# Reordering the second stage of a fused attention and feed-forward kernel: scaling of w_out among block transposes, an earlier load of batch 2's v, and second scores one step later

## The chip, the cores and the metric

The kernel runs on one core of a Trainium2 chip. The metric is the device time of one execution in microseconds (us); the profiled span is about 2 us shorter (287.1 against 288.98 us here). The engines are named as in the profile: PE is the matrix engine (PEld its weight loads), DVE is VectorE, ACT is ScalarE, POOL is GpSimd, SP is SyncE. A "q" after a name means the engine's sequencer, which also issues DMAs.

## The reference, cut to what matters

```python
# attention inside chunks of 64 tokens: 8 batches, 8 heads, 576 tokens, head size 64
scores = scale * np.matmul(q_c, k_c.transpose(0, 1, 2, 4, 3))
attn = softmax(scores)                       # written out in the reference
out = np.matmul(attn, v_c)
x = out.transpose(0, 2, 1, 3).reshape(4608, 512)
# feed-forward: w_in is 512 x 2048, w_out is 2048 x 512
h = x @ w_in
g = h * (1.0 / (1.0 + np.exp(-beta * h)))
return g @ w_out
```

## The kernel before

The tokens go through in nine blocks of 512. For each block PE does a long run of hidden-layer matmuls (`hps`), then the output product. Between them lie the scores (`sc`, 64 tiny matmuls of 32 rows by 64 columns for each group of four chunks) and the attention products (`x`) of the next block. From block 1 on, the output product is a Strassen-like form which needs four precomputed differences of w_out (`tw`); block 0 uses the plain form in 16 units of four wide matmuls: unit number 4g + t uses quarter g of w_out.

Because the activation is written as Silu of beta times h, w_out must be divided by beta first. That is `scale_w_out(g)`, four VectorE instructions for quarter g, called "group g" below. GpSimd issues all loads (they convert float32 to float16 on the way: the page gives 36.71 MB read from HBM and 18.35 MB carried by the loads' queue, q0) and calculates the differences.

```python
def scale_w_out(g):                                    # VectorE, 4 instructions of 128x512 f16
    for kk in range(4 * g, 4 * g + 4):
        nc.vector.tensor_scalar_mul(wo(kk), wo(kk), binv[:, kk % 2, kk // 2:kk // 2 + 1])

def T_items(b):                                        # VectorE: 4 block transposes, q and k of batch b
    return [lambda z=z, w=w: emit_T(b, z, w) for z in range(2) for w in range(2)]

def emit_tw(n):                                        # GpSimd: one weight difference, 128x2048 f16
    # ... tw1 = b12 - b11 (needs groups 0 and 1), tw2 = b22 - tw1 (needs all), tw4 = b21 - tw2, tw3 = b22 - b12
    nc.gpsimd.tensor_tensor(out=o, in0=a_, in1=b_, op=ALU.subtract)
# ...
load_w_out(0); load_w_out(1)                           # one call per line in the kernel
load_qk(1)
load_w_out(2)
load_v(1)
load_w_out(3)
load_qk(2)
# ... attention of block 0, then the hidden layer of block 0:
L1(0, {-2: lambda: emit_xp(2), -3: lambda: emit_xp(3)}, 4)
scale_w_out(0)
scale_w_out(1)
for f in T_items(1):
    f()
scale_w_out(2)
scale_w_out(3)
emit_tw(1)
emit_tw(2)
load_v(2)
load_qk(3)
emit_tw(4)
emit_tw(3)
hooks = {
    9: lambda: emit_sc(2),
    11: lambda: emit_sc(3),
    12: lambda: emit_pv(4, xbar=False),                # attention product, then VectorE normalises it
    13: lambda: [emit_pv(5, xbar=False), emit_xp(4)],
    14: lambda: [emit_pv(6, xbar=False), emit_xp(5)],
    15: lambda: [emit_pv(7, xbar=False), emit_xp(6)],
}
for kk, f in enumerate(L2_plain(0)):                   # the 16 units of block 0's output product
    hooks.get(kk, lambda: None)()
    f()
# ... blocks 1 to 8
```

In the traces of this case each engine runs its instructions in the order in which the program names them (VectorE, for example, starts the four transposes at 33.05, 35.82, 36.92 and 38.00 us and then group 2 of the scaling at 39.08). The order of calls above is therefore the order on each engine.

The softmax here doesn't subtract the row's maximum and nothing guards it: scores larger than these inputs give would overflow.

Of the kernel before, what the change touches and what calls it, by code (L numbers as in the profile page):

```python
# [15 lines left out]
def kernel(  # L16
# [10 lines left out]
    nc = tc.nc  # L27
# [88 lines left out]
    def scale_w_out(g):  # L116
        for kk in range(4 * g, 4 * g + 4):
            nc.vector.tensor_scalar_mul(wo(kk), wo(kk), binv[:, kk % 2, kk // 2:kk // 2 + 1])  # L118
# [15 lines left out]
    def T_items(b):  # L134
        return [lambda z=z, w=w: emit_T(b, z, w) for z in range(2) for w in range(2)]
# [35 lines left out]
    def emit_pv(i, spare=False, xbar=True):  # L171
        g = i // 2
        if spare:
            xs = [ps_p.tile([128, 4, 128], FP32, tag="p", name="xp") for _ in range(2)]
        else:
            x = ps_x.tile([128, 2, 4, 128], FP32, tag="x", name="x")
            xs = [x[:, 0], x[:, 1]]
        for s in range(4):
            z, a2 = s // 2, s % 2
            for hp, cp in ((0, 0), (1, 1), (0, 1), (1, 0)):  # L180
                b, cb = divmod(2 * i + cp, NCB)
                p0, o0 = 64 * hp, 64 * cp
                nc.tensor.matmul(  # L183
                    out=xs[hp][o0:o0 + 64, s, 0:D + 1],
                    lhsT=et_t[g, a2][p0:p0 + 64, z, 2 * (i % 2) + cp, :],
                    rhs=vbuf[b % NV][p0:p0 + 64, s, cb, 0:D + 1],
                )
        rd = rd_p.tile([128, 2, 4, 1], FP32, tag="rd", name="rd")
        x16 = x_p.tile([128, 2, 4, D], FP16, tag="x16", name="x16")
        for xx, rr, yy in (  # L190
            [(xs[h], rd[:, h], x16[:, h]) for h in range(2)] if spare else [(x, rd, x16)]
        ):
            shape = [128] + list(yy.shape[1:])
            if spare:
                nc.vector.reciprocal(out=rr, in_=xx[:, :, D:D + 1])
                src = xx[:, :, 0:D]
            else:
                nc.vector.reciprocal(out=rr, in_=xx[:, :, :, D:D + 1])
                src = xx[:, :, :, 0:D]
            nc.vector.tensor_tensor(  # L200
                out=yy, in0=src, in1=rr.to_broadcast(shape), op=ALU.mult,
            )
        j, t0 = i // 4, (i % 4) * 128
        if j not in xt_t:
            xt_t[j] = xt_p.tile([128, KDM, BLK], FP16, tag="xt", name="xt")
        xf = x16.rearrange("p e s d -> p (e s d)")
        if xbar:
            nc.sync.dma_start_transpose(out=xt_t[j][:, :, t0:t0 + 128], in_=xf)
        else:
            x16_t[i] = xf  # L210

    def emit_xp(i):
        xf = x16_t.pop(i)
        j, t0 = i // 4, (i % 4) * 128
        xps = ps_s.tile([128, KDM, 128], FP16, tag=f"sc{i % 2}", name="xps")
        for kk in range(KDM):
            nc.tensor.transpose(
                out=xps[:, kk, :], in_=xf[:, kk * 128:(kk + 1) * 128], identity=ident
            )
        nc.scalar.copy(out=xt_t[j][:, :, t0:t0 + 128], in_=xps)  # L220

    def emit_idle(n):
        d = ps_p.tile([128, BLK], FP32, tag="p", name="idle")
        for _ in range(n):
            nc.tensor.matmul(out=d, lhsT=zero[:, 0:128], rhs=zero, start=True, stop=True)

    gt_t = {}
    s_t = {}
# [49 lines left out]
    def emit_tw(n):  # L278
        t1, t2, t3, t4 = tw
        w = w_out16.rearrange("p m r d -> p (m r) d")  # L280
        b11, b12 = w[:, 0:NM, 0:HM], w[:, 0:NM, HM:DM]
        b21, b22 = w[:, NM:KFF, 0:HM], w[:, NM:KFF, HM:DM]
        o, a_, b_ = {1: (t1, b12, b11), 2: (t2, b22, t1), 3: (t3, b22, b12), 4: (t4, b21, t2)}[n]
        nc.gpsimd.tensor_tensor(out=o, in0=a_, in1=b_, op=ALU.subtract)
# [172 lines left out]
    with tc.manual_schedule():  # L457
        load_qk(0, split=True)
        nc.vector.memset(zero, 0.0)
        nc.vector.memset(bstage, 0.0)  # L460
        nc.vector.memset(warm, 0.0)
        nc.scalar.activation(out=warm, in_=warm, func=ACTF.Exp, scale=1.0)
        for g4 in range(4):
            nc.sync.dma_start(
                out=bstage[32 * g4:32 * g4 + NM].rearrange("p r i -> p (r i)"),
                in_=moe_beta.rearrange("(m g x) -> g m x", g=4, x=64)[g4],
            )
        for t in vbuf:
            nc.vector.memset(t[:, :, :, D:D + 1], 1.0)
        load_v(0)  # L470
        make_identity(nc, ident)
        for g in range(4):
            load_w_in(g)
        load_w_out(0)
        load_w_out(1)
# [6 lines that stand above are left out]
        emit_idle(4)  # L482
        for f in T_items(0):
            f()
        nc.vector.transpose(
            out=bt, in_=bstage.rearrange("p r i -> p (r i)").rearrange("p (i r) -> p r i", r=2)
        )
        eps = 2.0 ** -10
        nc.vector.tensor_tensor(out=bm, in0=bt, in1=bt, op=ALU.mult)
        nc.vector.tensor_scalar(  # L490
            out=bm, in0=bm, scalar1=eps * eps, scalar2=None, op0=ALU.is_ge)
        nc.vector.scalar_tensor_tensor(
            out=beta2, in0=bt, scalar=eps, in1=bm, op0=ALU.subtract, op1=ALU.mult)
        nc.vector.tensor_scalar_add(beta2, beta2, eps)
        nc.vector.reciprocal(out=binv, in_=beta2)
        emit_sc(0, between=lambda: emit_idle(5))
        emit_sc(1, spare=True)
        emit_idle(3)
        emit_pv(0, xbar=False)
        emit_pv(1, spare=True, xbar=False)  # L500
        emit_xp(0)
        emit_pv(2, xbar=False)
        emit_xp(1)
        emit_pv(3, spare=True, xbar=False)

        L1(0, {-2: lambda: emit_xp(2), -3: lambda: emit_xp(3)}, 4)
        scale_w_out(0)
        scale_w_out(1)
        for f in T_items(1):
            f()  # L510
        scale_w_out(2)
        scale_w_out(3)
        emit_tw(1)
        emit_tw(2)
        load_v(2)
        load_qk(3)
        emit_tw(4)
        emit_tw(3)
        hooks = {
            9: lambda: emit_sc(2),  # L520
            11: lambda: emit_sc(3),
            12: lambda: emit_pv(4, xbar=False),
            13: lambda: [emit_pv(5, xbar=False), emit_xp(4)],
            14: lambda: [emit_pv(6, xbar=False), emit_xp(5)],
            15: lambda: [emit_pv(7, xbar=False), emit_xp(6)],
        }
        for kk, f in enumerate(L2_plain(0)):
            hooks.get(kk, lambda: None)()
            f()

        for j in range(1, NB):
            na = j + 1
            hooks = {}
            if na < NB:
                hooks[KFF] = lambda: emit_sc(2 * na)
            if j == 1:
                T2 = T_items(2)
                hooks.update({-1: lambda: emit_xp(7), 4: T2[0], 7: T2[1], 10: T2[2], 12: T2[3]})
            L1(j, hooks)
            at = []  # L540
            if na < NB:
                at = [
                    lambda: emit_pv(4 * na), lambda: emit_sc(2 * na + 1),
                    lambda: emit_pv(4 * na + 1), lambda: emit_pv(4 * na + 2),
                    lambda: emit_pv(4 * na + 3),
                ]
            tr = T_items(j + 2) if j + 2 < B else []

            def go(lst):
                if lst:  # L550
                    lst.pop(0)()

            mm, cB, cD, cC = steps_L2(j, last=(j == NB - 1))
            mm[0]()
            while fill:
                dve()
            mm[1]()
            cB()
            go(at)
            go(at)  # L560
            emit_sum(j, 4, 0)
            emit_sum(j, 4, 1)
            mm[2]()
            go(tr)
            go(at)
            emit_sum(j, 4, 2)
            emit_sum(j, 4, 3)
            mm[3]()
            go(at)
            go(tr)  # L570
            mm[4]()
            cD()
            go(at)
            go(tr)
            mm[5]()
            if j < NB - 1:
                cC()
            go(tr)
            mm[6]()
            if j + 2 < B:  # L580
                load_v(j + 2)
            if j + 3 < B:
                load_qk(j + 3)
# [30 lines left out]
```

## Time and profile before

| | before |
|---|---|
| median time | 288.98 us (288.88 to 289.02, 4 runs) |
| profiled span | 287.1 us, granted clock 1.00 |
| PE busy | 271.6 us, 95% |
| start of block 0's hidden layer | 17.83 us |
| start of block 1's long hidden-layer run | 55.44 us |
| from there to the end | 231.6 us, PE back to back nearly throughout |

The first lines of the profile's page, and its line for queue 8, which it names instruction:

```profile
span 287.1 us, 7722 instructions
PE 271.6 (95%) x3388; PEld 176.4 (61%) x3388; DVE 140.6 (49%) x261; ACT 161.8 (56%) x240; POOL 117.1 (41%) x114
...
q8 instruction: 26, 0.43, 0.6%
```

The 26 packets of queue 8 carry 0.43 MB, so about 16 KB each.

The waits of PE in the first 100 us. Columns: engine and line that waited, who released it, us in total, times, longest:

```profile
PE sc L155 <- DVE kT L127: 5.4, 1, 5.4
PE ops L405 <- DVE w_out L118: 1.5, 1, 1.5
...
PE x L183 <- issue: 0.6, 1, 0.6
PE sc L155 <- ACT et L164: 0.5, 2, 0.3
```

The change is aimed at the last three. "Issue" means that PE waited for nothing that the profile knows of.

The timeline of the stage. Columns: start, duration, engine, line, operation, count, and in brackets the idle time before it and what ended it. Lines of weight loads (PEld) are left out here and below without a mark; "..." stands for all other lines left out:

```profile
37.04 4.07 POOL L284 TENSOR_TENSOR tw<-w_out 128x2048 f16<-128x2048 f16 x1
...
39.08 2.99 DVE L118 TENSOR_SCALAR w_out<-w_out,binv 128x512 f16<-128x512 f16 x4
41.33 1.16 PE L405 MATMUL ops<-w_out,gt 128*128 128x512 f16 x4 [1.47 <-DVE w_out L118]
...
44.55 1.14 DVE L118 TENSOR_SCALAR w_out<-w_out,binv 128x512 f16<-128x512 f16 x4 [2.49 <-DMA w_out<-in_moe_w_out_dram]
...
47.26 0.22 PE L183 MATMUL x<-vb,et 64*64 64x65 f16 x3
48.05 0.31 PE L183 MATMUL x<-vb,et 64*64 64x65 f16 x13 [0.56 <-issue]
48.29 1.04 PE L405 MATMUL ops<-w_out,gt 128*128 128x512 f16 x4
...
49.46 0.32 PE L183 MATMUL x<-vb,et 64*64 64x65 f16 x16
```

Group 2 of the scaling (39.08) takes 2.99 us for the same four instructions that take 1.14 us as group 3 (44.55). In the trace its first instruction alone lasts 2.20 us and ends at 41.28, which is 0.17 us after GpSimd's difference ends. PE starts unit 8 at 41.33, after 1.47 us of idleness. Unit 12, the first to use the last quarter of w_out, starts at 48.29.

The chain of waits through the same time (start, us, what):

```profile
39.23 2.06 DVE w_out L118
...
41.33 1.16 PE ops L405 x4
...
47.48 0.56 issue
48.05 0.41 PE x L183 x13
...
55.44 13.12 PE hps L240 x64
```

The cut in the middle holds the first scores, a table load of ScalarE (1.28 us from 43.23) and the exps (44.53 to 45.62), for which the second scores waited.

### The profile page before, as it was taken

The page shows a single profiled execution, that of the slowest core. Times are in us where ns is not written, and L with a number is a line of the kernel's source. Part 1 is how long each engine was busy: PE and PEld are TensorE (multiplying, and loading weights), DVE is VectorE, ACT ScalarE, POOL GpSimd, SP SyncE. Part 2 cuts the span into 40 slices and gives each one's busy share as a digit, 9 for nine tenths or more (in the row PEclk, how much of TensorE's full clock was granted, in tenths as well). Part 3 has the DMA queues.
Part 4 walks back from the last instruction along what each step waited for, and adds up shares of the span by engine and source line. Part 5 has one row for each costly group of instructions (what it writes and reads, how often), then busy time and mean ns, then how long its engine had stood idle before and what let it go on. Part 6 is the DMA issues. An engine that isn't in the chain of part 4 may idle for free.

```text
span 287.1 us, 7722 instructions
## 1 busy us (share of the span) xinstructions
PE 271.6 (95%) x3388; PEld 176.4 (61%) x3388; DVE 140.6 (49%) x261; ACT 161.8 (56%) x240; POOL 117.1 (41%) x114
## 2 busy tenths in 40 slices
PE   2779978999999999999999999999999999999995
PEld 0454434546874688468845884588458845885584
DVE  2751483837770677067806680668055404540433
ACT  2249505688348833883388438842884288518710
POOL 8733266994049203920393039302910260016100
PEclk9999999999999999999999999999999999999999
DMA  6999998990239626972597259823902320242013
GB/s 112 177 206 212 211 182 153 184 211 3 75 110 158 130 67 112 159 132 63 105 161 142 59 99 164 154 59 94 154 4 57 94 73 2 57 94 73 2 37 110
DMA packets 69584, 31.95 MB, mean 111 GB/s; under 512 B 53680, under 2 KB 63920, under 8 KB 69552
## 3 DMA queue, kind: packets, MB, share of 16 engines
q0 software_dynamic: 44960, 18.35, 51.9%
q1 hardware_dynamic: 24448, 12.99, 17.4%
q8 instruction: 26, 0.43, 0.6%
q10 hardware_dynamic: 144, 0.13, 0.1%
q14 instruction: 6, 0.05, 0.1%
HBM read 36.71 MB, written 9.44 MB: 161 GB/s over the span
## 4 chain that ended last, share of the span: by engine, by line
PE 82%; DMA 10%; DVE 3%; POOL 2%; issue 1%; ACT 1%; DVEq 0%; POOLq 0%; ACTq 0%
PE hps L240 39%; PE oA L310 20%; DMA ku<-in_k_dram 7%; PE oD L310 5%; PE oB L310 5%; PE oC L310 5%; PE sc L155 4%; PE x L183 3%; DMA vb<-in_v_dram 3%; PE ops L405 1%; DVE kT L127 1%; DVE w_out L118 1%; POOL qu L85 1%; PE oE L310 1%; POOL vb L95 1%
## 5 line engine op out<-in xcount | busy, mean ns | idle before, releaser
L240 PE MATMUL hps<-xt,wi 128*128 128x512 f16 (+1 forms) x656 | 127.8, 353 | 1.2 <-DMA wi<-in_moe_w_in_dram 0.7
L250 ACT ACTIVATE gt<-hps,beta 128x512 f16<-128x512 f32 x144 | 95.8, 688 | 17.8 <-PE hps L240 17.1
L240 PEld LDWEIGHTS <-wi 128*128 128x128 f16 x656 | 63.4, 98 | 61.7 <-DMA xt<-x 1.5
L270 DVE TENSOR_TENSOR s<-gt 128x512 f16<-128x512 f16 x32 | 17.7, 552 | 80.1 <-ACT gt L250 79.9
L355 POOL TENSOR_TENSOR w<-u,u 128x512 f32<-128x512 f32 x7 | 8.9, 1270 | 103.3 <-ACT u L321 103.3
L310 PEld LDWEIGHTS <-s 128*128 128x128 f16 x496 | 46.8, 98 | 6.0
L310 PE MATMUL oA<-tw,s 128*128 128x256 f16 x368 | 44.1, 273 | 0.0
L274 POOL TENSOR_TENSOR s<-gt 128x512 f16<-128x512 f16 x32 | 37.5, 1228 | 4.8 <-ACT gt L250 4.8
L310 PEld LDWEIGHTS <-gt 128*128 128x128 f16 x384 | 36.4, 98 | 4.8
L321 ACT COPY u<-oA 128x512 f32<-128x512 f32 x24 | 14.1, 588 | 37.0 <-PE oA L310 37.0
L164 ACT ACTIVATE et<-sc 128x512 f16<-128x512 f32 x34 | 18.5, 595 | 22.3 <-PE sc L155 22.2
L95 POOL DMA_DIRECT2D vb<-in_v_dram x32 | 27.5, 879 | 6.6 <-DMA wi<-in_moe_w_in_dram 5.0
L200 DVE TENSOR_TENSOR x<-x,rd 128x512 f16<-128x512 f32 x34 | 23.5, 691 | 1.3
L127 DVE STREAM_TRANSPOSE qT<-qu 128x576 f32<-128x576 f32 x16 | 20.0, 1250 | 5.8 <-DMA qu<-in_q_dram 5.8
L127 DVE STREAM_TRANSPOSE kT<-ku 128x576 f32<-128x576 f32 x16 | 19.9, 1241 | 2.1 <-DMA ku<-in_k_dram 2.0
L155 PEld LDWEIGHTS <-kT 32*64 32x64 f16 x1152 | 11.6, 111 | 12.2 <-DVE kT L127 6.3
L155 PE MATMUL sc<-qT,kT 32*64 32x64 f16 x1088 | 12.8, 195 | 6.2 <-DVE kT L127 5.4
L272 DVE TENSOR_TENSOR s<-s,gt 128x512 f16<-128x512 f16 x32 | 17.8, 555 | 1.1
L372 ACT COPY o<-oA 128x512 f32<-128x512 f32 x7 | 4.1, 586 | 23.2 <-PE oA L310 23.2
L405 PE MATMUL ops<-w_out,gt 128*128 128x512 f16 x64 | 15.3, 379 | 1.5 <-DVE w_out L118 1.5
L375 POOL TENSOR_TENSOR o<-t,o 128x512 f32<-128x512 f32 x7 | 8.9, 1270 | 18.0 <-ACT o L372 18.0
L164 ACT ACT_TABLE_LOAD x8 | 10.3, 1283 | 10.0 <-PE sc L155 9.9
(56 smaller groups left out, 208.8 us busy)
## 6 DMA issues: line engine op xcount, KB each, us to landing
out_dram<-osb SPq DMA_DIRECT2D x21, 256.0 KB, 2.2
vb<-in_v_dram POOLq DMA_DIRECT2D x32, 144.0 KB, 4.9
qu<-in_q_dram POOLq DMA_DIRECT2D x7, 576.0 KB, 9.1
ku<-in_k_dram POOLq DMA_DIRECT2D x7, 576.0 KB, 11.1
out_dram<-o SPq DMA_DIRECT2D x14, 256.0 KB, 2.2
wi<-in_moe_w_in_dram POOLq DMA_DIRECT2D x4, 512.0 KB, 12.5
w_out<-in_moe_w_out_dram POOLq DMA_DIRECT2D x4, 512.0 KB, 16.8
qu<-in_q_dram POOLq DMA_DIRECT2D x2, 288.0 KB, 5.3
```

The costliest lines, as they stand in the source:

```text
L95: nc.gpsimd.dma_start(out=t[64 * hp:64 * hp + 64, 2 * z:2 * z + 2, :, 0:D].rearrange("p s c d -> p (s c) d"), in_=v[b, h0:h0 + 2].rearrang ...
L127: nc.vector.transpose(out=dst[b][:, z].rearrange("p t r e -> p (t r e)").bitcast(FP32).rearrange("p (t r) -> p r t", r=RUN), in_=src[b][:, ...
L155: nc.tensor.matmul(out=sc[a % 2][o0:o0 + 64, z, c, :], lhsT=kk[:, cb * CH:(cb + 1) * CH, e], rhs=qq[:, cb * CH:(cb + 1) * CH, e], start=(e ...
L164: nc.scalar.activation(out=et, in_=sc[s], func=ACTF.Exp, scale=scale)
L200: nc.vector.tensor_tensor(out=yy, in0=src, in1=rr.to_broadcast(shape), op=ALU.mult,)
L240: nc.tensor.matmul(out=hps_t[j, m][:, c0:c1], lhsT=w_r[m // 4][:, 2 * z + e, m // 2 % 2, m % 2, :], rhs=xt_t[j][:, n, c0:c1], start=(n == ...
L250: nc.scalar.activation(out=gt_t[j][:, m, :], in_=hps, func=ACTF.Silu, scale=beta2[:, m % 2, m // 2:m // 2 + 1],)
L270: tt(out=s1[:, lo], in0=g[:, lo, dn], in1=g[:, hi, dn], op=ALU.add)
L272: tt(out=s2[:, lo], in0=s1[:, lo], in1=g[:, lo, up], op=ALU.subtract)
L274: tt(out=s3[:, lo], in0=g[:, lo, up], in1=g[:, lo, dn], op=ALU.subtract)
L310: nc.tensor.matmul(out=bank[name][:, i, :], lhsT=a[:, kk, i * 128:(i + 1) * 128], rhs=b[:, kk, :], start=(first and i == 0 and kk == 0), s ...
L405: nc.tensor.matmul(out=ops[t], lhsT=gt_t[j][:, kk, t * 128:(t + 1) * 128], rhs=wo(kk), start=(kk == 0), stop=(kk == KFF - 1),)
```

## The change

The intent, as far as the code tells it: let group 2 be scaled as soon as its weights have landed rather than after all four transposes of batch 1; get batch 2's v into the load queue earlier; and move the second scores of block 1 behind the first attention product, so that they need not wait for the exps of the first scores. Four idle matmuls are added in the start-up.

```diff
-    def emit_idle(n):
+    def emit_idle(n, w=512):
         d = ps_p.tile([128, BLK], FP32, tag="p", name="idle")
         for _ in range(n):
-            nc.tensor.matmul(out=d, lhsT=zero[:, 0:128], rhs=zero, start=True, stop=True)
+            nc.tensor.matmul(
+                out=d[:, 0:w], lhsT=zero[:, 0:128], rhs=zero[:, 0:w], start=True, stop=True)
@@
         emit_pv(1, spare=True, xbar=False)
+        emit_idle(4, 256)
         emit_xp(0)
@@
-        for f in T_items(1):
-            f()
+        T1 = T_items(1)
+        T1[0]()
+        T1[1]()
         scale_w_out(2)
+        T1[2]()
+        T1[3]()
         scale_w_out(3)
+        load_v(2)
         emit_tw(1)
+        load_qk(3)
         emit_tw(2)
-        load_v(2)
-        load_qk(3)
         emit_tw(4)
         emit_tw(3)
@@
-            11: lambda: emit_sc(3),
-            12: lambda: emit_pv(4, xbar=False),
+            12: lambda: [emit_pv(4, xbar=False), emit_sc(3)],
```

## The prediction

> **What bounds the kernel now.** The page gives PE 271.6 us of the 287.1 us span, granted clock full in every slice. In the chain of waits, from 55.4 us on, PE work follows PE work almost to the end; nothing moved here can shorten that. The loss is before. PE's waits in the first 100 us: 5.4 for the first transposes, 0.7 for w_in (17.8), 1.5 of the first output product for the scaled w_out (41.3), 0.5 of the second scores for the exps, 0.6 inside the first attention product, labelled "issue". Between 39.9 and 55.4 PE idles about 4 us in all.

> **Why 41.3.** The timeline: VectorE's third scaling group stands behind four transposes (the last ends at 39.2). Its first instruction takes 2.20 us where others take 0.35, ending 0.17 us after GpSimd's weight difference (37.04 to 41.11). [...]

> **What the change does** (order of the built instructions, durations of the trace):
> - Scaling group 2 waits for its load, not for all transposes: issue 18.07 + 20.2 us to landing = 38.3. Done by about 39.5.
> - v of batch 2 goes before the first difference; its four issues each wait for an older load (landing 38.3, 39.2, 40.2, 41.1), so the difference runs 42.0 to 46.1. Group 2 is clear of it: the 1.5 us go.
> - The last two transposes move to about 39.5 to 41.8. The first scores of block 1 need them: PE waits about 0.6 us halfway through.
> - Second scores after the first attention product: their 0.5 us wait for the exps and the 0.6 us go.
> - The cost: scaling group 3's weights land at 44.56 (before, GpSimd was idle then). [...] group 3's first instruction should take about 1.7 us and end at 46.3. PE, otherwise ready at 45.8 for the last quarter of the output product, starts it at 46.3 (before 48.3).
> - VectorE's normalising of the first attention product stands behind group 3: 0.8 + 0.2 + 0.7 us, so the next attention product starts at 48.1 instead of 49.5, PE waiting about 0.6 us. From there the old chain, about 1.4 us earlier.
> - Four idle matmuls of 256 columns (about 0.45 us) fill a 0.9 us gap at 14.6; the start at 17.8 waits for w_in and the clock is full: nothing.
> - The later differences end at about 59.9 instead of 62.8; slack either way.

> **On the critical path:** of about 2.6 us of waits removed, about 1.2 come back, so 1.4 us net: 287.6 us. Range 286.5 to 288.6. Faster by over 2%: 0.01; within 2%: 0.98; slower: 0.01.

> **What would show it.** Timeline: group 2 from 38.3, each under 0.5 us; first difference near 42.0; group 3's first instruction ending at 46.2; the long run of hidden-layer matmuls of block 1 starting near 54.0 instead of 55.44; the rest of the chain as long as before; first hidden layer still at 17.8.

> **What would make it wrong.** If the lock doesn't catch group 3, the gain is up to 2.6 us, 286.4. If the v issues hold group 2 for a whole issue (0.85 us) each, or the scores wait longer for the transposes, it sinks to 0.5 us. If batch 2's early v delays w_out's last quarter in the DMA rings, the gain goes.

"The lock", here and below, is only a name for what the traces show: a VectorE instruction of the scaling that meets GpSimd's difference ends just after it (in the kernel before, group 2's first instruction took 2.20 us where others take 0.35, and ended 0.17 us after the difference). The 1.7 us and the 46.3 us for group 3 are estimates from that: weights at 44.56, the difference until 46.1, and about 0.2 us more.

## The result, and the profile after

The changed kernel takes 287.9 us (median of 4 runs, 287.56 to 288.05) against 288.98 us before. The ratio is 0.9962, with a 95% interval of 0.9944 to 0.9979. Ratios here and below are the mean time of one kernel's fast runs over the mean of the other's in the same rounds on the same chip, so they are not quite the ratio of the medians quoted. The profiled run's span is 286.1 us, against 287.1.

The page of the changed kernel:

```profile
span 286.1 us, 7731 instructions
PE 272.1 (95%) x3392; PEld 176.9 (62%) x3392; DVE 139.8 (49%) x261; ACT 161.8 (57%) x240; POOL 116.9 (41%) x114
```

The waits of PE in its first 100 us:

```profile
PE sc L155 <- DVE kT L127: 6.0, 2, 5.6
...
PE x L183 <- DVE x L200: 0.6, 2, 0.5
...
PE ops L406 <- DVE w_out L118: 0.5, 1, 0.5
...
PE sc L155 <- issue: 0.2, 1, 0.2
```

The wait for the scaled w_out is 0.5 us instead of 1.5, the wait of the scores for the exps is gone, and "issue" has gone from 0.6 us inside an attention product to 0.2 us inside the scores. New are a wait for a transpose (the second of the two waits in the first line) and a wait of 0.5 us for the normalised attention product.

The timeline of the stage in the changed kernel:

```profile
38.22 1.47 DVE L118 TENSOR_SCALAR w_out<-w_out,binv 128x512 f16<-128x512 f16 x4 [1.39 <-DMA w_out<-in_moe_w_out_dram]
...
39.96 2.55 POOL L95 DMA_DIRECT2D vb<-in_v_dram  x3 [0.61 <-issue]
...
42.00 0.38 PE L155 MATMUL sc<-qT,kT 32*64 32x64 f16 x24 [0.41 <-DVE kT L127]
...
42.52 4.07 POOL L285 TENSOR_TENSOR tw<-w_out 128x2048 f16<-128x2048 f16 x1
...
44.32 3.28 DVE L118 TENSOR_SCALAR w_out<-w_out,binv 128x512 f16<-128x512 f16 x4 [2.38 <-DMA w_out<-in_moe_w_out_dram]
...
46.81 1.23 PE L406 MATMUL ops<-w_out,gt 128*128 128x512 f16 x4 [0.45 <-DVE w_out L118]
...
48.50 0.32 PE L183 MATMUL x<-vb,et 64*64 64x65 f16 x16 [0.47 <-DVE x L200]
```

Group 2 now runs at 38.22, clear of the difference. Group 3, which took 1.14 us before, takes 3.28 us: its first instruction alone lasts 2.43 us in the trace and ends at 46.75, which is 0.16 us after the difference (42.52 to 46.59). The stretched scaling has moved from group 2 to group 3.

The chain of waits says the same:

```profile
30.23 14.07 DMA w_out<-in_moe_w_out_dram
...
44.32 3.28 DVE w_out L118 x4
...
48.50 0.32 PE x L183 x16
...
54.49 13.12 PE hps L241 x64
```

The changed kernel's critical path leads from the landing of the last quarter of w_out through the held group 3 and the normalising to the second attention product. The long run starts at 54.49 instead of 55.44, 0.95 us earlier, and from there to the end it is 231.6 us in both; the spans differ by 0.93 us. So all of the gain is won before the long run.

### The profile page after: what moved, and what is told of

The parts are those of the page before. It is cut to its first block, busy times and chain, and to the rows that moved or that the text cites. A ratio compares the mean times of both kernels' runs of the same rounds, so it can differ in the third digit from the quotient of the medians.

```text
span 286.1 us, 7731 instructions
## 1 busy us (share of the span) xinstructions
PE 272.1 (95%) x3392; PEld 176.9 (62%) x3392; DVE 139.8 (49%) x261; ACT 161.8 (57%) x240; POOL 116.9 (41%) x114
## 4 chain that ended last, share of the span: by engine, by line
PE 80%; DMA 14%; DVE 3%; POOL 1%; issue 1%; ACT 0%; DVEq 0%; POOLq 0%
PE hps L241 39%; PE oA L311 20%; DMA w_out<-in_moe_w_out_dram 11%; PE oD L311 5%; PE oB L311 5%; PE oC L311 5%; PE sc L155 3%; DMA vb<-in_v_dram 3%; PE x L183 3%; DVE w_out L118 1%; PE oE L311 1%; PE ops L406 1%; DVE x L200 0%; POOL qu L85 0%; POOL ku L85 0%
## 5 line engine op out<-in xcount | busy, mean ns | idle before, releaser
L251 ACT ACTIVATE gt<-hps,beta 128x512 f16<-128x512 f32 x144 | 95.8, 688 | 17.8 <-PE hps L241 17.1
L271 DVE TENSOR_TENSOR s<-gt 128x512 f16<-128x512 f16 x32 | 16.2, 507 | 81.4 <-ACT gt L251 81.4
L311 PEld LDWEIGHTS <-s 128*128 128x128 f16 x496 | 46.8, 98 | 6.0
L273 DVE TENSOR_TENSOR s<-s,gt 128x512 f16<-128x512 f16 x32 | 17.8, 555 | 1.1
L330 DVE TENSOR_TENSOR osb<-oB,u 128x512 f32<-128x512 f32 x8 | 5.5, 691 | 20.8 <-PE oB L311 20.8
```

Of the source, the lines that this page charges most:

```text
L251: nc.scalar.activation(out=gt_t[j][:, m, :], in_=hps, func=ACTF.Silu, scale=beta2[:, m % 2, m // 2:m // 2 + 1],)
L271: tt(out=s1[:, lo], in0=g[:, lo, dn], in1=g[:, hi, dn], op=ALU.add)
L273: tt(out=s2[:, lo], in0=s1[:, lo], in1=g[:, lo, up], op=ALU.subtract)
L311: nc.tensor.matmul(out=bank[name][:, i, :], lhsT=a[:, kk, i * 128:(i + 1) * 128], rhs=b[:, kk, :], start=(first and i == 0 and kk == 0), s ...
```

## The experiments

Twelve kernels ran, all correct. Each had five or six timed runs against the kernel before, on the same chip.

| run | median us | before us | ratio | 95% interval |
|---|---|---|---|---|
| the change | 287.9 | 288.98 | 0.9962 | 0.9944 to 0.9979 |
| scaling_only | 289.74 | 288.95 | 1.0031 | 1.0019 to 1.0044 |
| loads_only | 288.14 | 288.95 | 0.9974 | 0.9962 to 0.9987 |
| scores_only | 288.79 | 288.95 | 0.9997 | 0.9984 to 1.0009 |
| no_idle | 288.03 | 288.95 | 0.9976 | 0.9962 to 0.9989 |
| halves | 288.19 | 288.95 | 0.9973 | 0.9960 to 0.9987 |
| diff3_first | 287.28 | 288.95 | 0.9934 | 0.9921 to 0.9947 |
| diff3_first_T_first | 287.28 | 288.95 | 0.9939 | 0.9927 to 0.9952 |
| scores_shift | 288.60 | 288.95 | 0.9986 | 0.9974 to 0.9999 |
| scores_shift64 | 289.53 | 288.71 | 1.0028 | 1.0016 to 1.0041 |
| best_shift64 | 291.23 | 288.71 | 1.0082 | 1.0062 to 1.0103 |
| wout_early | 290.70 | 288.71 | 1.0063 | 1.0039 to 1.0087 |
| scores_apart | 287.27 | 288.76 | 0.9941 | 0.9927 to 0.9954 |

### The parts of the change, one by one

**scaling_only**: the kernel before, with the new place of the scaling alone.

```diff
-        for f in T_items(1):
-            f()
-        scale_w_out(2)
-        scale_w_out(3)
+        T1 = T_items(1)
+        T1[0](); T1[1](); scale_w_out(2); T1[2](); T1[3](); scale_w_out(3)
```

> The kernel before plus only the new place of scaling groups 2 and 3 among the transposes of batch 1. Theory [...]: the difference still runs 37.0 to 41.1, so the first instruction of group 2, released at 38.2, ends at 41.3 all the same; the last two transposes then end near 44.2 instead of 39.2 and the first scores of block 1 wait for them. Slower than before: about 290.2 us, span of the stage to the long hidden-layer run about 1.2 us longer. Rival (the scaling was late because it stood behind four transposes): group 2 done by 39.5, the 1.5 us wait gone, 287.5 us.

It got slower, by 0.3%. Its timeline:

```profile
36.94 4.07 POOL L284 TENSOR_TENSOR tw<-w_out 128x2048 f16<-128x2048 f16 x1
...
38.18 3.79 DVE L118 TENSOR_SCALAR w_out<-w_out,binv 128x512 f16<-128x512 f16 x4 [1.20 <-DMA w_out<-in_moe_w_out_dram]
```

Group 2 starts 0.9 us earlier than in the kernel before and ends no earlier: its first instruction lasts until 41.17, 0.16 us after the difference. So the queue of transposes ahead of it was not what made it late; the difference on GpSimd was. The last two transposes are late instead, and the first scores wait 1.43 us for them. The rival falls. The loss was 0.8 us, somewhat less than the 1.2 expected. Not all of it need be waiting: in the profiled run, the slowest of the five (290.23 us), the granted clock also fell to 0.50 from 43.7 to 47.1 us. The one run with a granted clock of 1.00 took 289.48 us, still more than the highest of the kernel before (289.21).

**loads_only**: the kernel before, with only the loads moved ahead of the differences.

```diff
+        load_v(2)
         emit_tw(1)
+        load_qk(3)
         emit_tw(2)
-        load_v(2)
-        load_qk(3)
```

> The kernel before plus only batch 2's loads moved ahead of the differences. Theory: the difference starts near 42.3, group 2 runs unhindered right after the four transposes (39.1 to 40.2), no wait of PE for it and none for the transposes; group 3 (weights land at 44.3) is then held by the difference until about 46.5, as in the changed kernel. The scores' own wait for the exps stays. About 287.9 us, the same as the changed kernel within 0.3. [...] Rival (place among the transposes matters): kept at 289.0.

It takes 288.14 us, within 0.3 of the changed kernel. From its timeline:

```profile
39.28 1.27 DVE L118 TENSOR_SCALAR w_out<-w_out,binv 128x512 f16<-128x512 f16 x4
...
44.75 3.33 DVE L118 TENSOR_SCALAR w_out<-w_out,binv 128x512 f16<-128x512 f16 x4 [4.20 <-DMA w_out<-in_moe_w_out_dram]
```

Group 2 runs at 39.28 in 1.27 us, right behind the four transposes, and PE doesn't wait for it. Group 3 starts at 44.75 and takes 3.33 us behind a difference that starts at 42.98. So moving the loads accounts for most of the change's gain, and the new place among the transposes is not needed for it. The second v issue came at 40.44. Whether VectorE's scaling or the older load that it waits for sets the gap before it (0.6 us in the changed kernel) was a second question of this run, and 40.4 was the number written down for the scaling. But the scaling doesn't explain it: in the nine kernels with batch 2's v ahead of the differences it comes 0.81 to 0.82 us after the landing of the load it waits for, whether the scaling has ended (at 39.69 in the changed kernel, with the issue at 39.96) or still runs (to 40.55 here). Why 0.8 us, where GpSimd's other waits for a load mostly ended 0.28 to 0.54 us after the landing, stays open.

**scores_only**: the kernel before, with only the second scores moved.

```diff
-            11: lambda: emit_sc(3),
-            12: lambda: emit_pv(4, xbar=False),
+            12: lambda: [emit_pv(4, xbar=False), emit_sc(3)],
```

> The kernel before plus only the second scores one step back. Theory: the 1.5 us wait at 41.3 stays, but group 3 is done at 45.7 with GpSimd idle, so once the waits around the second scores (0.5) and in the first attention product (0.6) are gone, PE reaches the last quarter of the output product at about 46.7 instead of 48.3, and the attention product after it at 47.6 instead of 49.5: about 287.1 us, which is better than the whole change. Rival (the waits at the scores are a small matter and the scaling is what counts): 288.5 us or more.

This was wrong: 288.79 us and no significant gain. The waits around the scores did go away, but another came in their place. From its waits of PE:

```profile
PE sc L155 <- issue: 1.3, 1, 1.3
```

and from its timeline:

```profile
45.91 0.60 PE L155 MATMUL sc<-qT,kT 32*64 32x64 f16 x51
...
47.80 0.31 PE L155 MATMUL sc<-qT,kT 32*64 32x64 f16 x13 [1.28 <-issue]
```

PE stops for 1.28 us after 51 of 64 identical tiny matmuls, with nothing to wait for that the profile shows. What that is was the question of the later runs.

**no_idle**: the changed kernel without the four added idle matmuls.

```diff
-        emit_idle(4, 256)
```

> The changed kernel without the four idle matmuls of 256 columns. Theory: they fill a gap and the clock is full, so 287.9 us, equal to the changed kernel within 0.2 us. Rival: they delay the first hidden layer by their 0.45 us, which would show as 0.3 to 0.5 us less without them; or they keep the clock up, which would show as more time and a granted clock under 1.00 between 14 and 20 us.

The time is the same within 0.2 us, as expected, but part of my reasoning was not right: without them the clock did fall in the profiled run. The table by stretches, first of no_idle and then of the changed kernel (columns: stretch, length, busy time and count of PE, PEld, DVE, ACT and POOL, granted clock, DMA share, GB/s):

```profile
16.00:18.00 2.00, 1.39 (x41) 0.94 (x40) 1.90 (x7) 1.17 (x2) 0.70 (x1) 0.83 1.21 199
18.00:20.00 2.00, 2.00 (x12) 1.48 (x12) 0.80 (x3) 0.00 (x0) 0.00 (x0) 0.50 1.24 206
20.00:22.00 2.00, 1.76 (x16) 1.33 (x15) 0.00 (x0) 1.35 (x3) 0.88 (x1) 0.82 1.27 214
```

```profile
18.00:20.00 2.00, 1.73 (x20) 1.59 (x20) 1.12 (x5) 0.66 (x2) 0.00 (x0) 1.00 1.24 206
```

In no_idle the granted clock was 0.83, 0.50 and 0.82 in the three stretches; in the changed kernel it was 1.00 in all three. In this stretch the clock also fell in scores_only (0.66 from 18 to 20 us, 0.50 from 20 to 22), though not in the kernel before, scaling_only or loads_only, none of which has the added matmuls (the first eight hidden-layer matmuls took 1.05, 1.03 and 1.05 us there, 1.86 in no_idle). The wait of the first attention product for v doesn't sort them: the profile lists none for no_idle, 0.55 us in scaling_only and 0.87 us in scores_only. Nor is a long stop of PE seen ahead of it: in no_idle PE never stood longer than 0.91 us between 9 us and the fall at 17.31. What decides it is open. The loss doesn't reach the end, as the two traces show: block 0's output product started 1.0 us later in no_idle (34.22 us, 33.22 in the changed kernel) and so did unit 8 (41.12, 40.12), but unit 12 started at 46.75 against 46.81, since PE waited for group 3 there in both.

### The lock

**halves**: the changed kernel with its first difference cut into two instructions.

```diff
-        emit_tw(1)
+        emit_tw(1, (0, 4))      # columns of the first half of the tile
+        emit_tw(1, (4, 8))
```

> The changed kernel with its first weight difference cut into two GpSimd instructions of half the columns, the same work. [...] halves run about 42.5 to 44.6 and 44.6 to 46.6; the first scaling of group 3, released at 44.3, ends near 44.8 (46.8 in the changed kernel), the next one only near 46.8, behind the second half. The last one still ends near 47.5, so the time hardly moves: 287.8 us, within 0.3 of the changed kernel. Rival (the two engines share the bandwidth, or group 3 waits for something else): the first scaling still ends near 46.7, as in the changed kernel.

The time did what was expected. The detail did not:

```profile
42.54 4.21 POOL L286 TENSOR_TENSOR tw<-w_out 128x1024 f16<-128x1024 f16 x2
...
44.38 3.40 DVE L118 TENSOR_SCALAR w_out<-w_out,binv 128x512 f16<-128x512 f16 x4 [2.30 <-DMA w_out<-in_moe_w_out_dram]
```

The second half starts at 44.63 in the trace, although group 3 had been ready since 44.38. Group 3's first instruction ends at 46.91, again 0.16 us after GpSimd's last (46.75). So in this run the boundary between the two differences let the waiting VectorE instruction in no sooner; the expectation that it would slip in between the halves fell, and the rival's number, 46.7, was nearly met. The rival's reason, shared bandwidth, does not fit the traces: in all nine kernels where an instruction of the scaling was held (for 2.20 us in the kernel before, 3.0 in scaling_only and 2.43 in the changed kernel, against 0.35 unheld), it ends 0.16 to 0.17 us after GpSimd's. In no_idle the weights landed a microsecond later, at 45.28, so that group 3's first instruction was held for 1.39 us and not for 2.43; it ended 0.16 us after the difference (46.54) all the same. And the difference takes no longer beside a held instruction (4.07 us in the changed kernel) than without one (4.06 us in diff3_first, below).

**diff3_first**: the changed kernel with an order in which no difference can run before group 3, because the third difference needs group 3 and stands first.

```diff
         load_v(2)
-        emit_tw(1)
         load_qk(3)
+        emit_tw(3)
+        emit_tw(1)
         emit_tw(2)
         emit_tw(4)
-        emit_tw(3)
```

> The changed kernel with both of batch 2's loads first and the third difference, which needs group 3 itself, ahead of the others; so no difference can run before group 3 is scaled. Theory (the lock on group 3 is what eats the gain): group 3 runs 44.3 to 45.5, PE starts the last quarter of the output product near 46.3 instead of 46.8 and the attention product after it near 47.2 instead of 48.5: 286.6 us, 1.3 under the changed kernel. Rival (PE is held by loads or scores anyway): 287.9 us, unchanged.

It takes 287.28 us: 0.6 us less than the changed kernel, about half of what was expected.

```profile
45.65 1.31 DVE L118 TENSOR_SCALAR w_out<-w_out,binv 128x512 f16<-128x512 f16 x4 [3.69 <-DMA w_out<-in_moe_w_out_dram]
...
46.30 1.10 PE L406 MATMUL ops<-w_out,gt 128*128 128x512 f16 x4
...
47.86 0.32 PE L183 MATMUL x<-vb,et 64*64 64x65 f16 x16 [0.46 <-DVE x L200]
```

Group 3 takes 1.31 us instead of 3.28, and unit 12 starts at 46.30, as expected. The reason why the second attention product started at 47.86 and not 47.2 is that in the profiled run the last quarter of w_out landed at 45.63, not 44.3 as in the changed kernel. The five times are 286.50, 286.62, 287.28, 287.35 and 287.51; two of them meet the expectation, and the profiled one is among the others. Whether the landing is what divides them can't be told, since one run only was profiled. The edit also changes a second thing: batch 3's q is now issued at 42.57 us instead of 46.53, ahead of that landing. It needn't be the cause of the late landing, since no_idle, with the old order of the loads, had 45.28 and diff3_first_T_first, with the new one, 44.74; but no run separates the two edits.

**diff3_first_T_first**: the same, and the transposes of batch 1 all before group 2, as in the kernel before.

```diff
-        T1[0](); T1[1](); scale_w_out(2); T1[2](); T1[3](); scale_w_out(3)
+        for f in T_items(1):
+            f()
+        scale_w_out(2)
+        scale_w_out(3)
```

> The same with the old order on VectorE, all four transposes before group 2. Theory: with GpSimd out of the way until group 3, the place among the transposes is not needed; group 2 ends near 40.3, in time, and the scores don't wait for a transpose (0.4 us in the changed kernel), PE about 0.6 us earlier there: 286.0 us. The second scores then run into the arrival of PE's next block of instructions near 45.3, which costs a few tenths. Rival (the scaling must stand between the transposes): slower than the run diff3_first, 287 us or more.

It takes 287.28 us, no less and no more. Group 2 was in time, so the rival, that the scaling must stand between the transposes, falls. But what PE won there it lost to the stop in the second scores, now 1.38 us:

```profile
PE sc L155 <- issue: 1.4, 1, 1.4
```

### The stop labelled "issue"

In the profiles with such a stop, I counted PE's instructions (each weight load and each matmul is one) up to it, and looked up the 16 KB packets of queue 8, which the page names instruction, among the trace's DMA packets. The page doesn't say whose queue it is: PE runs 6776 weight loads and matmuls in the kernel before, and no other engine as many as 300, so queue 8 is taken to be PE's. Its 26 packets would then carry about 260 of PE's instructions each (6776 over 26), an estimate. The three places where PE stops in these runs, after 446, 958 and 1214 instructions, lie 512 and 256 apart; 256 instructions are called a block below, and 704 and 960 are the borders of one, estimated from the stop at 958.

**scores_shift**: scores_only with eight more idle matmuls, so sixteen more PE instructions, at the very start.

```diff
-        emit_idle(4)
+        emit_idle(12)
         for f in T_items(0):
```

> The run scores_only again, with eight more idle matmuls of 512 columns at the very start, where PE waits anyway. In scores_only PE stood for 1.28 us in the middle of the second scores, labelled issue; counted in its program, that was at instruction 960 or so, the same place as the gap labelled issue in the kernel before, although other work stands there, and it ended 1.5 us after a 16 KB packet of the instruction queue. Theory (PE ran out of fetched instructions, and the fetch is asked for at a fixed place in the program, near instruction 820): sixteen more instructions ahead move the request about 1.7 us earlier in the work, so the packet starts near 43.5 and there is no gap, PE reaches the last quarter of the output product near 46.8 instead of 48.0: 287.5 us. Rival (the scores wait for something of their own: a buffer, a load): the gap stays in the same matmul, 288.8 us.

```
run                   passes 704   packet of queue 8   stop at   PE resumes   after packet's end
before                42.55        45.63 to 46.53      958       48.05        1.52
scores_only           42.46        45.36 to 46.26      958       47.80        1.54
scores_shift          42.44        45.24 to 46.13      958       47.55        1.42
loads_only            41.04        44.12 to 45.01      958       46.54        1.53
changed kernel        41.18        43.52 to 44.41      958       46.01        1.60
diff3_first_T_first   41.36        44.33 to 45.23      958       46.80        1.57
diff3_first           41.24        43.55 to 44.44      958       46.02        1.58
scores_shift64        (earlier)    15.47 to 16.43      446       17.74        1.31
best_shift64          (earlier)    15.89 to 16.85      446       18.24        1.39
wout_early            (earlier)    15.45 to 16.40      446       17.73        1.33
scores_apart          40.20        41.72 to 42.63      no stop   -            -
no_idle               42.21        43.16 to 44.09      no stop   -            -
scores_shift64        39.40        39.21 to 40.10      none here -            -
```

The stops lie at 958, and in three kernels at 446, which is 512 instructions, two blocks, earlier. Wherever PE stops it resumes 1.3 to 1.6 us after a packet ends. That holds for a third place too: in best_shift64 PE also stopped for 0.44 us at instruction 1214, one block after 958, and resumed at 54.19, 1.48 us after a packet (51.20 to 52.71). Where PE stops at 958, the packet begins 2.3 to 3.1 us after PE has passed instruction 704, one block before the stop. So in these kernels it is about 5 us from passing 704 until the next block can be used (2.3 to 3.1, plus 0.9 for the packet, plus 1.5), an estimate put together from these rows. But 704 is not shown to be the place where the block is asked for: the packet began 0.95 us after it in no_idle, 1.5 us in scores_apart, and in scores_shift64 0.2 us before PE reached it. What starts the packet is open. The block from 704 to 960 holds most of 64 tiny matmuls of the first scores, three units of wide matmuls, 16 attention matmuls and most of the second scores. PE runs through them in less than that: in scores_only from 42.46 to 46.33.

In the kernel before, PE also waited for the exps inside this block, and what was left showed as the 0.56 us in the attention product. The prediction booked those two waits as separate savings. They are one budget: less waiting for the exps is more waiting for instructions (0.51 and 0.56 us before; none and 1.28 us in scores_only).

**scores_shift64**: scores_only with 64 more instructions at the start, so that the block boundaries fall elsewhere.

```diff
         emit_idle(4)
+        emit_idle(32, 128)
         for f in T_items(0):
```

> The run scores_only with 64 more instructions of PE at the very start (32 idle matmuls of 128 columns, while PE waits for the first transposes). The two runs before showed that the gap moves with the count of instructions (eight matmuls earlier for sixteen instructions) but that the 16 KB packet of the instruction queue came at nearly the same time, 45.24 against 45.36. So the request is not near instruction 820; a request [...] near 704, would fit: that is the start of the first scores in all these kernels, and packets start 2.3 to 3.0 us later. Theory: 64 more instructions put that request four quarter-products earlier, about 38 us, the packet before 42, no gap in the second scores; PE reaches the last quarter of the output product near 46.7 instead of 48.0 and the next attention product near 47.6 instead of 49.0: 287.4 us. Rival (the gap belongs to the second scores themselves): 288.7 us.

**best_shift64**: diff3_first_T_first with the same added line.

> The run diff3_first_T_first, where PE stood 1.38 us in the second scores, with the same 64 instructions at the start. Theory: no gap; the last quarter of the output product starts near 45.6 instead of 47.1, the attention product after it near 47.0 instead of 48.0, when VectorE has normalised the one before: 286.2 us. Rival: 287.3 us, unchanged.

In both the stop in the second scores was gone, as expected: the packet came at 39.2 and 39.5, before those scores, and PE went through them without a gap. In both the time got worse, 289.53 and 291.23 us. The waits of PE in scores_shift64 show where a stop went:

```profile
PE x L183 <- issue: 1.8, 1, 1.8
```

The shift put an earlier boundary, after 446 instructions, into the attention products of the start-up, and PE stopped there for 1.84 and 1.53 us. The clock fell as well (0.53 and 0.50 between 20 and 22 us), so block 0's run of 64 hidden-layer matmuls started at 22.94 and 23.36 us; that was 20.86 in the changed kernel. In both, PE also waited later for the transposing loads of the next blocks, 1.3 and 2.7 us in total, which it did not in the changed kernel; why is open. These two runs test the place of the stop; their times say nothing of what its removal is worth.

**wout_early**: best_shift64 with the last quarter of w_out loaded before batch 1's v, and the differences in their old order after the loads.

```diff
-        load_v(1)
         load_w_out(3)
+        load_v(1)
```

> best_shift64 with the last quarter of w_out loaded ahead of batch 1's v, and the differences in their old order after the loads. Theory: the quarter lands near 40.6, group 3 is scaled by 42, and VectorE is free to normalise the first attention product as soon as v has landed (44.5): next attention product near 46.3, 285.6 us. If v landing later holds PE instead, 286.2 us, as best_shift64.

It takes 290.70 us and suffers from the same stop at 446 (1.4 us) as the kernel that it was built on, so its time tells nothing of its own question, which is left open. The first steps of its theory held (the quarter landed at 40.50 and group 3 was done by 41.66), but the second attention product started at 48.58 us, not 46.3.

**scores_apart**: diff3_first_T_first without additions at the start; instead, wide matmuls are put between the two sets of scores.

```diff
-            9: lambda: emit_sc(2),
-            12: lambda: [emit_pv(4, xbar=False), emit_sc(3)],
-            13: lambda: [emit_pv(5, xbar=False), emit_xp(4)],
+            8: lambda: emit_sc(2),
+            12: lambda: emit_pv(4, xbar=False),
+            13: lambda: [emit_sc(3), emit_pv(5, xbar=False), emit_xp(4)],
```

> The run diff3_first_T_first, with nothing added at the start, but the first scores before the third quarter of the output product instead of one unit into it, and the second scores after the first unit of the last quarter instead of before it. The 64 added instructions of the two runs before removed the gap in the second scores but put an earlier block boundary of PE's program into the early attention products (1.8 and 1.5 us of waiting at instruction 446) and lowered the clock. Theory [...]: here the block from 704 to 960 holds three or four more units of wide matmuls between its ends, the request comes about 0.9 us earlier, and no gap of more than 0.2 us is left in the second scores. The last quarter of the output product starts near 45.2, the second attention product near 47.0 instead of 48.0, when VectorE has normalised the first: 286.3 us, up to 287.2 in runs where the last quarter of w_out lands late. Rival (the second scores wait wherever they stand): 287.3 us.

No stop is left; the timeline shows all 64 second scores in one piece:

```profile
44.98 1.31 DVE L118 TENSOR_SCALAR w_out<-w_out,binv 128x512 f16<-128x512 f16 x4 [4.82 <-DMA w_out<-in_moe_w_out_dram]
45.39 1.34 PE L406 MATMUL ops<-w_out,gt 128*128 128x512 f16 x4 [0.80 <-DVE w_out L118]
...
46.66 0.71 PE L155 MATMUL sc<-qT,kT 32*64 32x64 f16 x64
...
47.30 0.32 PE L183 MATMUL x<-vb,et 64*64 64x65 f16 x16
```

The time is 287.27 us, not the 286.3 expected. The second attention product starts at 47.30, 0.7 us earlier than in diff3_first_T_first, but the transposes behind it then wait 0.52 us for the exps of the second scores, which now come later. PE also waits 0.80 us for group 3, and group 3 for its load, which landed at 44.96. With the lock and the instruction stop out of the way, what remains there is the arrival of the weights.

So three versions tie at 287.3 us, about 0.6% under the kernel before and 0.2% under the changed kernel. The intervals of diff3_first and of the change just overlap (0.9921 to 0.9947, 0.9944 to 0.9979), and they come from different rounds, so the second figure is likely and not established.

## Why the prediction was right or wrong

The prediction was 287.6 us with a range of 286.5 to 288.6; measured were 287.9. Point by point:

- *The bound.* Right. From the long run of block 1 on nothing changed (231.6 us in both), and all of the gain lies before it.
- *Group 2 from 38.3, done by about 39.5, and the 1.5 us go.* Right: 38.22 to 39.69, though one of its four instructions took 0.68 us and not under 0.5 (it ended 0.1 us after the first v issue). That it was the lock is what scaling_only (group 2's first instruction until 41.17, 0.16 us after the difference) and loads_only (group 2 in 1.27 us, before a difference that starts at 42.98) show. The prediction credited the place among the transposes and the moved loads together; the moved loads suffice.
- *The scores wait 0.6 us for a transpose.* Right, 0.4 us.
- *Group 3 falls under the difference and gives part of the gain back.* Right in kind. What it costs is seen in diff3_first, which is 0.6 us lower without it, with the doubts named there. The size was off by half a microsecond: the difference started at 42.52 and not 42.0, since the second v issue came only after a gap of 0.61 us, so group 3's first instruction ended at 46.75 instead of 46.3, unit 12 began at 46.81 instead of 46.3, and the second attention product at 48.50 instead of 48.1. The long run started at 54.49 instead of 54.0, and this term is nearly all of the difference between a predicted gain of 1.4 us and the measured 1.1.
- *The waits of 0.5 us for the exps and of 0.6 us labelled "issue" both go, because the second scores move.* Wrong as reasoning. The second is, by the counts above, a wait for instructions (it ends 1.3 to 1.6 us after a packet of queue 8), and it grows where PE hurries: moving the scores alone brought 1.28 us of it and no gain. In the changed kernel 0.19 us of it is left; PE would have waited for group 3 until 46.81 anyway. That it cost nothing there was luck of the prediction and not insight.
- *The idle matmuls do nothing.* Right for the time (288.03 without, 287.9 with). Not safe to say that the clock needs no help: without them it fell to 0.50 in the profiled runs of no_idle and scores_only, and stayed full in the start-up of the kernel before, scaling_only and loads_only, which don't have them either.
- *The first hidden layer starts at 17.8 still.* It started at 18.27 in the profiled run, after PE had waited 0.23 us for batch 0's v, which the change doesn't touch; the kernels scores_only and scaling_only, without the idle matmuls, have 18.22 and 18.20 too. The later start cost nothing here, since PE still waited 0.45 us for group 3 at 46.81.

## What to carry to other kernels

When a VectorE instruction takes several times its usual duration and ends with a GpSimd instruction (here 2.20 us instead of 0.35, ending 0.17 us after it), don't only move it away: see what the next VectorE instruction of the kind will meet at the new place, and make the GpSimd work depend on the last of them if it has time. A wait labelled "issue" inside a row of tiny matmuls should be counted in instructions: if it stays at the same count when instructions are added ahead (958 here, with sixteen added), PE is likely short of instructions, and wide matmuls between the tiny ones can take the stop away (they did in scores_apart, where the time stayed at 287.3 us because other waits took its place). Before adding waits up as savings, ask whether one of them hides another.
